# New order tables for a one-core hash-bucket attention and gated feed-forward kernel, and a mask kept in SBUF

## The chip, the cores and the metric

The kernel runs on one core of a Trainium2 chip. The time is that of one launch on the device, in microseconds (us): 607.29 us for the kernel before, the median of three runs (607.15 to 607.84). One more run was taken with the profiler on, and every duration below comes from that run.

## The reference

Four batches of eight attention heads, 768 positions, 64 numbers a head. Each query and key gets a 6-bit bucket from the signs of a projection; a query sees only keys of its own bucket. The heads' outputs are laid side by side (512 wide) and go through a gated feed-forward layer.

```
q_bits = (einsum('bhsd,dk->bhsk', q, proj) > 0)       # k likewise; 6 bits make a bucket
mask   = q_bucket[:, :, :, None] == k_bucket[:, :, None, :]
scores = where(mask, q @ k.T / sqrt(D), -1e9)
attn   = exp(scores - max); attn = attn / (sum + 1e-9)
x      = attn @ v, heads side by side                  # (4, 768, 512)
gate   = sigmoid(causal convolution of x over 5 positions, one filter per column)
out    = (gate * (x @ w_val)) @ w_out
```

## The kernel before

**Tiles.** A unit is one head of one batch (32 of them); a unit has six tiles of 128 queries, so there are 192 tiles, and 48 of them make a batch. One main loop (L521 to L560) runs over the tiles k = 0 to 195; it is called the step of tile k below. A step carries the tile through a chain that is spread over several steps.

**The chain of a tile.** TensorE (PE) makes the scores `s` in two pairs of matmuls (L295) into one of two PSUM buffers. VectorE (DVE) takes the negated row maximum `nm` (L301) and from it the factor `gs` (L307) and the shift `nb` (L311). ScalarE (ACT) makes `p` = exp (L317), with the row sum beside it; that frees the buffer of `s`. For two tiles at a time DVE adds the sums (L323) and takes the reciprocal `ri` (L327). GpSimd (POOL) scales `p` (L332). PE transposes `p` in six pieces into two PSUM buffers `tp` (L341), and ACT copies them to SBUF as `pt` (L350). With three tiles' `pt` a half of a head is complete; PE multiplies with the values (`av`, L364, one step of the generator is two matmuls), and ACT copies `av` into `x` (L372).

**What hangs on it.** For two heads together DVE rounds `x` to `xh` (L384), POOL takes the rest `xl` (L385), and the convolution runs as one POOL and four DVE instructions (L393, L395). After four pairs ACT makes the gates (L399) and the batch's feed-forward products can start: `val` (L426, 12 matmuls into `m`, in pieces of four) and `outp` (L451, also in pieces of four). They are held before a batch's last two output blocks until the next batch's gates are there (`hold`, L475). For a coming unit POOL rounds queries and keys (`aq` L207, `bq` L210), and once in four units PE makes the sign bits (L242, into a `tp` buffer, read by DVE at L245).

**The weights.** They come as 64-bit floats and are taken apart on DVE by five instructions of 128x512 for each of eight parts (L113, L114, L117, L120, L121), between L106 and L129 on ACT and L132 and L134 on POOL. `m` in these lines is one PSUM tile; ACT's output of L106 lies in the SBUF tile `o`.

**What sets the order.** Every engine executes its own instructions in the order in which the program issues them. That order is written by hand: each step has a string of letters, and each letter issues one piece. S scores of the next tile, M maximum, F factor, H shift, E exp, R and I sums and reciprocal, Z scaling, T transposes, K copy of the transposes of the step before, A one step of `av`, C one of the convolution, G one of the feed-forward products, P one of the preparation of a coming unit, W one of the weights. Tables before: FIRST for steps 0 to 5, EARLY (12 strings, step k takes number k mod 12) up to step 59, LATE (12 strings) from step 60 on. A letter whose generator has nothing left issues nothing. In steps up to 63 no G finds anything: the first batch's gates are not there.

```
 30 START = 60
522 o = FIRST[k] if k < 6 else EARLY[k % 12] if k < START else LATE[k % 12]
561 accs[:] = [(ps_m, "m"), (ps_t, "tp"), (ps_s, "s"), (ps_t, "tp"), (ps_s, "s")]
```

After the last step the products of the last batch run alone (L561 to L568), with more PSUM buffers.

Of the kernel before, what the change touches and what calls it, by code (L numbers as in the profile page):

```python
# [11 lines left out]
ALU = mybir.AluOpType  # L12
# [3 lines left out]
I32 = mybir.dt.int32  # L16
U32 = mybir.dt.uint32
# [9 lines left out]

START = 60  # L30
FIRST = ["SGKMRIWFWGTHWWEZ", "GMFRGHSICKWCEGZT", "MSRFIKHETZP",
         "RMSGCKIFCPHTEPGWPCZCPC", "MRFPSCKHEPGIPZCATGPAP", "ASAARAPMWPCFGIHCPKETZ"]
EARLY = ["MRFHCIKSETZ", "MRWIFKHEWGASGCGZT", "MRFKPSHPIPEPATZ",
         "RMKCIFHSAEZT", "MKFPHRIPPEPSCWWZWPTA", "MRFAKHSIWCPETZ",
         "MKRFISPPHEZWT", "MRFHSKAIZWACET", "MSGKCRFIHGWEATZG",
         "MRKIZFSAGCHACTEG", "MAFRIKHGSCWEPPPWPTZ", "MKRFSHPEIAZTW"]
LATE = ["MRKCAAFHISZECGT", "PMSRFPKHGIEATZW", "MFRWHISZCKEGGWWWT",
         "MWSWRICFKHEPPGAAZAPT", "MKFRSIZHCEPCPPGT", "SMFHKRIWWWZCCPGWWECT",
         "MWRPWFAHKIAEASTZ", "MSFWWKRHGEITWZ", "MFRKIHSPCEGWZWGTW",
         "MSRKAAPFIAHGZET", "MFKRSIHGZET", "PSMFKHRIEWCTPZ"]  # L40


@with_exitstack
def kernel(
# [10 lines left out]
    nc = tc.nc  # L55
# [53 lines left out]
    def from_float64(w, m, t):  # L109

        lo, hi = w[:, :, 0], w[:, :, 1]
        a, d, ti = hi.bitcast(FP32), lo.bitcast(FP32), t.bitcast(I32)
        nc.vector.tensor_scalar(out=t, in0=m, scalar1=LEAST, scalar2=None, op0=ALU.max)  # L113
        nc.vector.tensor_scalar(out=ti, in0=ti, scalar1=3, scalar2=0x3fffffff,  # L114
                                op0=ALU.logical_shift_left, op1=ALU.bitwise_and)
        yield
        nc.vector.scalar_tensor_tensor(out=hi, in0=hi, scalar=-2 ** 30, in1=ti,  # L117
                                       op0=ALU.bitwise_and, op1=ALU.bitwise_or)
        yield
        nc.vector.tensor_scalar(out=ti, in0=hi, scalar1=-2 ** 23, scalar2=None, op0=ALU.bitwise_and)  # L120
        nc.vector.scalar_tensor_tensor(out=d, in0=lo.bitcast(U32), scalar=2.0 ** -52, in1=t,  # L121
                                       op0=ALU.mult, op1=ALU.mult)
        return a, d

# [16 lines left out]
    def load_conv():  # L141
        if conv_w.dtype == mybir.dt.int64:
            w = const.tile([P, NP * KW, 2], I32, name="cw64")
            nc.sync.dma_start(out=w, in_=conv_w.bitcast(I32).rearrange("p (n t) -> p n t", t=2))
            t = const.tile([P, NP * KW], FP32, name="cwt")
            yield
            a, d = yield from from_float64(w, magnitudes(w, const.tile([P, NP * KW], FP32, name="cwm")), t)
            yield
            nc.vector.tensor_tensor(out=cw_sb, in0=d, in1=a, op=ALU.add)
        else:  # L150
            nc.sync.dma_start(out=cw_sb, in_=conv_w)
# [32 lines left out]
    def load_raw(i):  # L184
        if i < len(units):
            b, h = units[i]
            raws[i] = raw.tile([P, S], FP32, name="r")
            nc.sync.dma_start(out=raws[i], in_=qk[b, h])

    def load_values(i):  # L190
        b, h = units[i]
        if h % 2 == 0:
            vts[i] = vp.tile([P, KB, P], FP32, name="vt")
            nc.sync.dma_start(out=vts[i], in_=v[b, h // 2])
        else:
            vts[i] = vts[i - 1]
# [101 lines left out]
    def maxima(k):  # L298
        s = ss[k]
        nm = small.tile([P, 1], FP32, name="nm")  # L300
        nc.vector.tensor_reduce(out=nm, in_=s[:, :, 0:HS], axis=AX.XY, op=ALU.max, negate=True)  # L301
        nms[k] = nm
# [18 lines left out]
    def row_sums(k):  # L321
        sums[k] = small.tile([P, 2], FP32, name="s1")
        nc.vector.tensor_reduce(out=sums[k], in_=ps[k][1], axis=AX.X, op=ALU.add)  # L323
# [185 lines left out]
    with tc.manual_schedule(engines=ENGINES):  # L509
        for i in range(5):  # L510
            load_raw(i)
        load_values(0)
        first_prep()
        weights = [load_conv(), load_weights()]
        preps = [prep(1)]
        step(preps)
        scores(0)
        load_raw(5)
        next(weights[0])
        next(weights[1])  # L520
        for k in range(N + LAG + 1):  # L521
            o = FIRST[k] if k < 6 else EARLY[k % 12] if k < START else LATE[k % 12]
            for act in o:
                if act == "K" and 0 <= k - LAG - 1:
                    keep_transposed(k - LAG - 1)
                elif act == "M" and k < N:
                    maxima(k)
                elif act == "R" and k % 2 == 0 and 0 <= k - 2 < N:
                    row_sums(k - 2)
                elif act == "F" and k < N:  # L530
                    factors(k)
                elif act == "I" and k % 2 == 0 and 0 <= k - 2 < N:
# [95 lines left out]
```

## Time and profile before

| what | value |
|---|---|
| median of three runs | 607.29 us (607.15 to 607.84) |
| the profiled execution's own time | 606.39 us |
| its span, first to last instruction | 604.6 us |
| mean granted TensorE clock | 0.997 |
| instructions | 10636 |
| VectorE, busy share of the span | 68% |
| ScalarE, busy share | 70% |
| GpSimd, busy share | 64% |
| read from HBM, written | 23.12 MB, 6.29 MB |

The page gives the busy time of each engine and the waits between them; further views cut the span into stretches, list one engine's instructions in order of time with the idle time ahead of each, and list the instructions of one source line. In such a list a row is: start in us, duration in us, engine, line, operation, output<-inputs, shape, type, count; in square brackets stands idle time of that engine and what ended it. PE's ends are modelled, and a row's matmuls overlap the next row's, so PE's time is read from one row's start to the next row's start.

### The profile page before, as it was taken

How to read it: one execution, taken by the hardware profiler on the slowest of the kernel's cores; microseconds unless marked ns; L12 is line 12 of the kernel's file. 1: busy time of each engine (PE TensorE's matmuls, PEld its weight loads, DVE VectorE, ACT ScalarE, POOL GpSimd, SP SyncE). 2: the span in 40 equal slices, each digit the busy share in tenths (PEclk: the TensorE clock that was granted, in tenths of full speed). 3: DMA queues.
4: the chain of work that ended last, by engine and by line, in shares of the span. 5: the costliest groups of instructions: out<-in, count | busy, mean ns of one | idle time of the engine just before them, and what ended most of it. 6: DMA issues, size and time to landing. Idle time of an engine off the chain costs nothing.

```text
span 604.6 us, 10636 instructions
## 1 busy us (share of the span) xinstructions
PE 586.0 (97%) x3516; PEld 430.6 (71%) x3516; DVE 411.8 (68%) x1007; ACT 425.4 (70%) x891; POOL 386.1 (64%) x380
## 2 busy tenths in 40 slices
PE   6999999999999999999999999999999999999997
PEld 4766656565677777766667777677758777776886
DVE  5778898989855846776756876468575776654532
ACT  4888988798886677768877676676879676674300
POOL 5558887888947755685846677467764768454322
PEclk9899999999999999999999999999999999999999
DMA  8535454535322253424233333332524222200111
GB/s 288 160 85 140 109 156 118 146 91 142 83 62 77 58 142 101 111 50 139 67 104 85 80 111 89 96 90 58 143 44 115 46 63 65 63 19 1 53 52 52
DMA packets 23413, 56.76 MB, mean 94 GB/s; under 512 B 4312, under 2 KB 4568, under 8 KB 23360
## 3 DMA queue, kind: packets, MB, share of 16 engines
q1 hardware_dynamic: 23072, 55.93, 34.2%
q8 instruction: 28, 0.46, 0.3%
q14 instruction: 25, 0.20, 0.1%
q10 hardware_dynamic: 288, 0.17, 0.1%
HBM read 23.12 MB, written 6.29 MB: 49 GB/s over the span
## 4 chain that ended last, share of the span: by engine, by line
PE 76%; ACT 9%; DVE 5%; issue 4%; POOL 4%; DMA 2%; SPq 0%; POOLq 0%; ACTq 0%; DVEq 0%
PE av L364 19%; PE s L295 18%; PE tp L341 15%; PE m L451 8%; PE m L426 8%; ACT p L317 5%; ACT pt L350 2%; DVE nm L301 2%; PE tp L242 2%; DMA r<-in_qk_dram 2%; PE tp L426 1%; PE tp L451 1%; PE s L451 1%; POOL p L332 1%; PE s L426 1%
## 5 line engine op out<-in xcount | busy, mean ns | idle before, releaser
L332 POOL TENSOR_SCALAR p<-p,ri 128x768 f32<-128x768 f32 x192 | 199.8, 1049 | 94.7 <-ACT pt L350 39.4
L301 DVE TENSOR_REDUCE nm<-s 128x1 f32<-128x768 f32 x192 | 183.1, 953 | 81.2 <-PE s L295 80.8
L317 ACT ACTIVATE p<-s,nb,gs 128x768 f32<-128x768 f32 x192 | 192.5, 1003 | 39.0 <-DVE nb L311 32.4
L350 ACT COPY pt<-tp 128x384 f32<-128x384 f32 x384 | 165.4, 485 | 75.9 <-PE tp L341 74.4
L341 PEld LDWEIGHTS tp<-ident,p 128*128 128x128 f32 x1152 | 133.3, 141 | 43.1 <-issue 19.0
L341 PE MATMUL tp<-ident,p 128*128 128x128 f32 x1152 | 160.9, 276 | 2.3 <-ACT pt L350 1.2
L364 PE MATMUL av<-pt,vt 128*64 128x384 f32 x768 | 147.9, 499 | 0.0
L295 PE MATMUL s<-ak,aq 76*128 76x384 f32 x384 | 117.0, 385 | 10.8 <-ACT p L317 9.1
L295 PE MATMUL s<-bk,bq 128*128 128x384 f32 x384 | 99.7, 341 | 0.0
L364 PEld LDWEIGHTS av<-pt,vt 128*64 128x64 f32 x768 | 48.6, 136 | 58.9 <-issue 55.8
L295 PEld LDWEIGHTS s<-ak,aq 76*128 76x128 f32 x384 | 58.0, 190 | 42.2 <-ACT p L317 20.8
L437 POOL TENSOR_TENSOR hl<-ht,hh 128x384 fp32r<-128x384 f32 x32 | 33.6, 1050 | 67.0 <-DVE hh L435 67.0
L395 DVE SCALAR_TENSOR_TENSOR g<-x,cw_sb,g 128x768 f32<-128x768 f32 x64 | 71.9, 1123 | 2.6 <-POOL g L393 2.1
L295 PEld LDWEIGHTS s<-bk,bq 128*128 128x128 f32 x384 | 70.6, 191 | 0.0
L210 POOL TENSOR_TENSOR bq<-r,aq 128x768 fp32r<-128x768 f32 x31 | 57.4, 1852 | 0.9
L385 POOL TENSOR_TENSOR xl<-x,xh 128x384 fp32r<-128x384 f32 x32 | 31.8, 1012 | 30.6 <-DVE xh L384 24.5
L451 PE MATMUL m<-wo,hh 128*128 128x512 f32 x144 | 47.5, 399 | 0.0
L426 PE MATMUL m<-xh,wv 128*128 128x384 f32 x200 | 43.8, 343 | 0.2 <-DVE ht L431 0.2
L311 DVE TENSOR_SCALAR nb<-nm,gs 128x1 f32<-128x1 f32 x192 | 40.3, 210 | 4.5
L317 ACT ACTIVATION_READ_ACCUMULATOR p<-s,nb,gs 128x1 f32 x192 | 38.9, 202 | 0.0
L372 ACT COPY x<-av 64x384 f32<-64x384 f32 x64 | 30.3, 473 | 12.1 <-PE av L364 11.2
L426 PEld LDWEIGHTS m<-xh,wv 128*128 128x128 f32 x200 | 35.2, 188 | 4.3 <-DVE s L323 3.0
(92 smaller groups left out, 468.0 us busy)
## 6 DMA issues: line engine op xcount, KB each, us to landing
r<-in_qk_dram SPq DMA_DIRECT2D x32, 384.0 KB
vt<-in_v_dram SPq DMA_DIRECT2D x16, 384.0 KB
ak<-aq SPq DMA_DIRECT2D x31, 192.0 KB
bk<-aq SPq DMA_DIRECT2D x31, 192.0 KB
bk<-bq SPq DMA_DIRECT2D x31, 192.0 KB
bq<-aq SPq DMA_DIRECT2D x31, 192.0 KB
out_dram<-o SPq DMA_DIRECT2D x23, 256.0 KB
w<-in_w_val_dram SPq DMA_DIRECT2D x4, 512.0 KB
```

The costliest lines, as they stand in the source:

```text
L210: nc.gpsimd.tensor_tensor(out=bq, in0=r, in1=aq.bitcast(FP32), op=ALU.subtract)
L295: nc.tensor.matmul(out=s[:, hf, 0:HS], lhsT=lq[0:n, qs], rhs=rk[0:n, hf * HS:(hf + 1) * HS], start=n == M, stop=n == P)
L301: nc.vector.tensor_reduce(out=nm, in_=s[:, :, 0:HS], axis=AX.XY, op=ALU.max, negate=True)
L311: nc.vector.tensor_scalar(out=nbs[k], in0=nms.pop(k), scalar1=gs[k], scalar2=None, op0=ALU.mult)
L317: nc.scalar.activation(out=p, in_=s[:, :, 0:HS], func=AF.Exp, bias=nb, scale=gs.pop(k), accum_out=sm[:, k % 2, 0:1])
L332: nc.gpsimd.tensor_scalar(out=p, in0=p, scalar1=rcs.pop(k), scalar2=1.0, op0=ALU.mult, op1=ALU.mult)
L341: nc.tensor.transpose(out=tp[:, n * P:(n + 1) * P], in_=p[:, kb * P:(kb + 1) * P], identity=ident)
L350: nc.scalar.copy(out=pt[:, :, qo:qo + P], in_=tp[:, 0:HS].rearrange("p (a b) -> p a b", b=P))
L364: nc.tensor.matmul(out=av[s * D:(s + 1) * D, 0:HS], lhsT=vt[:, kb, hh * D:(hh + 1) * D], rhs=pt[kb // 3][:, kb % 3, :], start=(kb == 0), s ...
L395: nc.vector.scalar_tensor_tensor(out=g, in0=x[:, k:k + S], scalar=w, in1=g, op0=ALU.mult, op1=ALU.add)
L426: nc.tensor.matmul(out=acc[:, 0:HS], lhsT=wv[wi][:, c, j * P:(j + 1) * P], rhs=xs_[(c, o)][xi], start=(m == 0), stop=(m == 11))
L451: nc.tensor.matmul(out=acc, lhsT=hs[(o, j)][hi][:, tb * P:(tb + 1) * P], rhs=wo[wi][:, j, :], start=(m == 0), stop=(m == 11))
```

## The change

All four tables' strings are new. A fourth table, TURN, is taken from step 60 on in the steps with 6 <= k mod 48 < 18, that is steps 60 to 65, 102 to 113 and 150 to 161; LATE holds for the other steps from 60 on. Apart from that, the mask of the weights' exponents (written by L120 and read by L121) goes into the SBUF tile that L106 wrote, no longer into the PSUM tile. The lines of the changed kernel are 5 higher from L120 on (8 higher behind the loop's head).

```diff
-LATE = ["MRKCAAFHISZECGT", "PMSRFPKHGIEATZW", "MFRWHISZCKEGGWWWT",
...
+LATE = ["MAKRFHAPISCEGTZ", "SKWWMRPPFHIGAZEAWWT", "MFSRKHICEGWGWWZT",
...
+TURN = ["MRKWFAHIEPCSZT", "WKSMGRPFHIAPWEZAWWT", "MFRWHCICPKEWPSWWWTZ",
...
-        nc.vector.tensor_scalar(out=ti, in0=hi, scalar1=-2 ** 23, scalar2=None, op0=ALU.bitwise_and)
-        nc.vector.scalar_tensor_tensor(out=d, in0=lo.bitcast(U32), scalar=2.0 ** -52, in1=t,
+        nc.vector.tensor_scalar(out=m.bitcast(I32), in0=hi, scalar1=-2 ** 23, scalar2=None, op0=ALU.bitwise_and)
+        nc.vector.scalar_tensor_tensor(out=d, in0=lo.bitcast(U32), scalar=2.0 ** -52, in1=m,
                                        op0=ALU.mult, op1=ALU.mult)
...
-            o = FIRST[k] if k < 6 else EARLY[k % 12] if k < START else LATE[k % 12]
+            if k < START:
+                o = FIRST[k] if k < 6 else EARLY[k % 12]
+            else:
+                o = TURN[k % 12] if 6 <= k % 48 < 18 else LATE[k % 12]
```

The work is the same on every engine: no instruction is added or taken away. What moves is shown at three places. On PE the rows of step k are here those from its scores (of tile k + 1) up to the next scores.

**Place one, PE, steps 114 to 116** (steps 6, 7 and 8 of LATE's twelve; `s` are scores, `tp` transposes, `m<-xh,wv` and `m<-xl,wv` pieces of `val`). Before:

```order
L295 MATMUL s<-ak,aq 128x384 x2
L295 MATMUL s<-bk,bq 128x384 x2
L341 MATMUL tp<-ident,p 128x128 x6
L295 MATMUL s<-ak,aq 128x384 x2
L295 MATMUL s<-bk,bq 128x384 x2
L426 MATMUL m<-xh,wv_126 128x384 x4
L341 MATMUL tp<-ident,p 128x128 x6
L295 MATMUL s<-ak,aq 128x384 x2
L295 MATMUL s<-bk,bq 128x384 x2
L426 MATMUL m<-xh,wv_127 128x384 x4
L426 MATMUL m<-xl,wv_126 128x384 x4
L341 MATMUL tp<-ident,p 128x128 x6
```

Now:

```order
L300 MATMUL s<-ak,aq 128x384 x2
L300 MATMUL s<-bk,bq 128x384 x2
L431 MATMUL m<-xh,wv_126 128x384 x4
L346 MATMUL tp<-ident,p 128x128 x6
L300 MATMUL s<-ak,aq 128x384 x2
L300 MATMUL s<-bk,bq 128x384 x2
L431 MATMUL m<-xh,wv_127 128x384 x4
L346 MATMUL tp<-ident,p 128x128 x6
L300 MATMUL s<-ak,aq 128x384 x2
L300 MATMUL s<-bk,bq 128x384 x2
L431 MATMUL m<-xl,wv_126 128x384 x4
L346 MATMUL tp<-ident,p 128x128 x6
```

The three pieces of `val` stood as none, one and two between the scores and the transposes of the three steps, and stand as one, one and one. The same happens at steps 66, 78, 90, 126, 138, 162, 174 and 186 with pieces of `val` or `outp`. A step that holds scores and transposes alone on PE is called bare below. From step 60 on there were 25 bare steps and are 16: the nine named here and step 61 are gone, and step 152, whose piece of `outp` moved, is new.

**Place two, DVE and POOL, steps 33 to 37** (EARLY; `g<-x` is the convolution, `xh` the rounding of `x`, `w` a part of the weights). DVE, from the maximum of tile 33 on. Before:

```order
L301 TENSOR_REDUCE nm<-s 128x1
L307 TENSOR_SCALAR gs<-nm 128x1
L395 SCALAR_TENSOR_TENSOR g<-x,cw_sb,g 128x768
L384 CAST xh<-x 128x384 x2
L311 TENSOR_SCALAR nb<-nm,gs 128x1
L301 TENSOR_REDUCE nm<-s 128x1
L307 TENSOR_SCALAR gs<-nm 128x1
L323 TENSOR_REDUCE s_1334<-sm_118 128x2
L327 RECIPROCAL ri<-s_1334 128x2
L311 TENSOR_SCALAR nb<-nm,gs 128x1
L120 TENSOR_SCALAR m<-w_1129 128x512
L121 SCALAR_TENSOR_TENSOR w_1129<-w_1129,m 128x512
```

Now:

```order
L306 TENSOR_REDUCE nm<-s 128x1
L312 TENSOR_SCALAR gs<-nm 128x1
L316 TENSOR_SCALAR nb<-nm,gs 128x1
L400 SCALAR_TENSOR_TENSOR g<-x,cw_sb,g 128x768
L389 CAST xh<-x 128x384 x2
L306 TENSOR_REDUCE nm<-s 128x1
L312 TENSOR_SCALAR gs<-nm 128x1
L328 TENSOR_REDUCE s_1338<-sm_118 128x2
L316 TENSOR_SCALAR nb<-nm,gs 128x1
L332 RECIPROCAL ri<-s_1338 128x2
L125 TENSOR_SCALAR o<-w_1121 128x512
L126 SCALAR_TENSOR_TENSOR w_1121<-w_1121,o 128x512
```

The shift `nb` of tile 33 stood behind a convolution instruction and two roundings, and stands in front of them; so it does in every step 9 of twelve in EARLY, and in step 3 of twelve it now stands in front of one convolution instruction. L120 now writes `o` and L121 reads it (L125 and L126 now). POOL at the same place, from the scaling of tile 32 (before) and of tile 32 (now) on; each `p<-p,ri` is the scaling of one tile. Before:

```order
L332 TENSOR_SCALAR p<-p,ri 128x768
L207 CAST aq<-r 128x768
L332 TENSOR_SCALAR p<-p,ri 128x768
L132 TENSOR_TENSOR w_1129<-w_1129,wv_126 128x512
L332 TENSOR_SCALAR p<-p,ri 128x768
L134 TENSOR_TENSOR wv_127<-w_1129 128x512
L393 TENSOR_SCALAR g<-x,cw_sb 128x768
L332 TENSOR_SCALAR p<-p,ri 128x768
L210 TENSOR_TENSOR bq<-r,aq 128x768
L368 MEMSET x 128x4
```

Now:

```order
L337 TENSOR_SCALAR p<-p,ri 128x768
L137 TENSOR_TENSOR w_1121<-w_1121,wv_126 128x512
L212 CAST aq<-r 128x768
L337 TENSOR_SCALAR p<-p,ri 128x768 x2
L139 TENSOR_TENSOR wv_127<-w_1121 128x512
L215 TENSOR_TENSOR bq<-r,aq 128x768
L398 TENSOR_SCALAR g<-x,cw_sb 128x768
L337 TENSOR_SCALAR p<-p,ri 128x768
L373 MEMSET x 128x4
```

The subtraction `bq` of 128x768 moved one scaling ahead: between two scalings there now stand the weights' L134 (L139), `bq` and the convolution's first product, where L134 and the product stood alone.

**Place three, PE, steps 109 to 111** (TURN; `tp<-r,proj_sb` are the sign bits, `av` attention times values). Before:

```order
L295 MATMUL s<-ak,aq 128x384 x2
L295 MATMUL s<-bk,bq 128x384 x2
L364 MATMUL av<-pt,vt 64x384 x2
L341 MATMUL tp<-ident,p 128x128 x6
L295 MATMUL s<-ak,aq 128x384 x2
L295 MATMUL s<-bk,bq 128x384 x2
L341 MATMUL tp<-ident,p 128x128 x6
L295 MATMUL s<-ak,aq 128x384 x2
L295 MATMUL s<-bk,bq 128x384 x2
L242 MATMUL tp<-r,proj_sb 32x384 x8
```

Now:

```order
L300 MATMUL s<-ak,aq 128x384 x2
L300 MATMUL s<-bk,bq 128x384 x2
L369 MATMUL av<-pt,vt 64x384 x4
L346 MATMUL tp<-ident,p 128x128 x6
L247 MATMUL tp<-r,proj_sb 32x384 x8
L300 MATMUL s<-ak,aq 128x384 x2
L300 MATMUL s<-bk,bq 128x384 x2
L346 MATMUL tp<-ident,p 128x128 x6
L300 MATMUL s<-ak,aq 128x384 x2
L300 MATMUL s<-bk,bq 128x384 x2
L369 MATMUL av<-pt,vt 64x384 x6
```

One step of `av` moved from step 107 to step 109, and the eight sign-bit matmuls from step 111 to the end of step 109, ahead of step 110's scores. At steps 157 to 159 the same rows stand. At steps 59 to 63 one step of `av` moved from 59 to 61, and the sign bits from 63 to either side of step 61's transposes.

More of the change, by code (lines that the diff above doesn't have):

```diff
@@ L30 @@
 START = 60
[L31 to L36, printed above, removed]
-LATE = ["MRKCAAFHISZECGT", "PMSRFPKHGIEATZW", "MFRWHISZCKEGGWWWT",
-         "MWSWRICFKHEPPGAAZAPT", "MKFRSIZHCEPCPPGT", "SMFHKRIWWWZCCPGWWECT",
-         "MWRPWFAHKIAEASTZ", "MSFWWKRHGEITWZ", "MFRKIHSPCEGWZWGTW",
-         "MSRKAAPFIAHGZET", "MFKRSIHGZET", "PSMFKHRIEWCTPZ"]
+FIRST = ["KRGGAGMCTIFHESZGG", "CMWRICKFHWETSWZG", "RCTMIWKFCWCSPCWPHZCWWEW",
+            "TMRFKIHESPPPZ", "RPMFTIAKAPASAAZGPHEPPPCPCPP", "MSRTIFWHCCKEZ"]
+EARLY = ["MFRHSKECGTIZG", "RWMAFIHKESPTCWZ", "MRFKHPISPEPPAPTZ",
+            "KMRFIHSTECZ", "KMFRHIEWPGAPZWWSPWPTPW", "MGRSGFGGGHIKACETZ",
+            "MGPRSFKGIHGZTE", "MRFHSGAIAKAWECZT", "MRKSFIHEPATGCZW",
+            "KMRIFSHAZAETACCP", "MFKRHIGWSEPZWGTPP", "MRKFHWIPGSPAETZ"]
+LATE = ["MAKRFHAPISCEGTZ", "SKWWMRPPFHIGAZEAWWT", "MFSRKHICEGWGWWZT",
+            "SWMKRIFHPWWEPAAPAPCGPWZT", "MKFRPSGHIPECTZ", "SRMKWFHWWIWPPWGPZWECWWT",
+            "MRKAFWPAHEIASGZTW", "SPWKMFRPPHIGETZ", "MRFKHPSIEWCGZT",
+            "SRKMFAACIPHZPGET", "MSKRFHIGETZ", "SKRIMFHECWTZ"]
+TURN = ["MRKWFAHIEPCSZT", "WKSMGRPFHIAPWEZAWT", "MFRWHCICPKEWPSWWWTZ",
+            "MSRFKIHCEPPPAAWAPPTZ", "MSRKFHICECGCTZ", "MRFSHWWKCWPWIWCWGCWPEWZCWT",
+            "MFRKAHIAEAGSTZ", "MKFSPPWRHIPEWTZ", "MFRHKGCEISZGWT",
+            "MKRSAAPFIAWPCHGEZT", "SMFGWRHIKWETZ", "MRPKGSFHIETZ"]
 @with_exitstack
```

## Prediction, made blind

> **What bounds the kernel now.** I read the page's first part, then the busy time by stretches, then the list of PE in order of time.
>
> ```profile
> PE 586.0 (97%) x3516; PEld 430.6 (71%) x3516; DVE 411.8 (68%) x1007; ACT 425.4 (70%) x891; POOL 386.1 (64%) x380
> ...
> 33.00:152.50 119.50, 116.04 (x697) 74.57 (x695) 108.42 (x258) 103.36 (x222) 94.72 (x93) 1.00 0.47 125
> ...
> 305.00:416.00 111.00, 111.00 (x690) 84.96 (x683) 71.51 (x180) 78.42 (x165) 68.67 (x66) 1.00 0.35 91
> ```
>
> A row of stretches has its length, then busy time of PE, PE's weight loads, DVE, ACT and POOL. Two different kernels lie in one span. From 305 to 416 us PE is busy all the 111.00 us and DVE 71.51: PE is the bound, and only time that PE loses there can be won. From 33 to 152.5 us (steps 12 to 58, EARLY) no feed-forward products exist yet; DVE has 108.42 of 119.50 us, PE's busy time is stretched by waits, and DVE is the bound.
>
> DVE's own waits in the early stretch, from the view of waits cut to it:
>
> ```profile
> DVE nm L301 <- PE s L295: 4.2, 10, 0.5
> DVE s L323 <- ACT p L317: 2.4, 9, 0.4
> ```
>
> So 6.6 us is what reordering alone could win there. Since PE hardly stands idle by its own busy time, its losses are read from start to start.
>
> **Part one: bare steps (place one).**
>
> ```profile
> 181.37 0.85 PE L341 MATMUL tp<-ident,p 128*128 128x128 f32 x6
> 182.64 0.62 PE L295 MATMUL s<-ak,aq 76*128 76x384 f32 x2 [0.42 <-ACT p L317]
> ...
> 318.97 0.62 PE L295 MATMUL s<-ak,aq 76*128 76x384 f32 x2
> 319.43 0.52 PE L295 MATMUL s<-bk,bq 128*128 128x384 f32 x2
> 319.79 0.81 PE L341 MATMUL tp<-ident,p 128*128 128x128 f32 x6
> 320.36 0.59 PE L295 MATMUL s<-ak,aq 76*128 76x384 f32 x2
> ...
> 321.85 0.82 PE L341 MATMUL tp<-ident,p 128*128 128x128 f32 x6
> 322.61 0.62 PE L295 MATMUL s<-ak,aq 76*128 76x384 f32 x2
> ...
> 535.13 0.82 PE L341 MATMUL tp<-ident,p 128*128 128x128 f32 x6
> 535.88 0.62 PE L295 MATMUL s<-ak,aq 76*128 76x384 f32 x2
> ```
>
> From the start of six transposes to the start of the next scores PE needs 320.36 - 319.79 = 0.57 us when nothing is late. The bare step 114 takes 320.36 - 318.97 = 1.39 us of PE, and in the step behind it the same stretch is 322.61 - 321.85 = 0.76: PE waits 0.19 for a score buffer. The reason is ACT's pace:
>
> ```profile
> 321.48 0.99 ACT L317 ACTIVATE p<-s,nb,gs 128x768 f32<-128x768 f32 x1
> 323.19 1.01 ACT L317 ACTIVATE p<-s,nb,gs 128x768 f32<-128x768 f32 x1
> ```
>
> From exp to exp ACT takes 323.19 - 321.48 = 1.71 us with no wait between, more than the 1.39 of a bare step. Step 115, with one piece of `val`, takes 322.61 - 320.36 - 0.19 = 2.06 us; with one piece in each of the three steps none is shorter, and ACT keeps up. Of the nine bare steps that vanish I count eight with a wait: 182.64 - 181.37 - 0.57 = 0.70 at the first (step 67's transposes) and about 0.19 at seven others, the last at 535.88 - 535.13 = 0.75. Together 0.70 + 7 x 0.19 = 2.0 us, won in stretches where PE is the bound, so nothing is late next but PE itself. The new bare step 152 gives some back: from nothing to the 0.70 of the first; I take 0.3.
>
> **Part two: the turns (place three).**
>
> ```profile
> 158.56 0.81 PE L341 MATMUL tp<-ident,p 128*128 128x128 f32 x6
> 159.99 0.61 PE L295 MATMUL s<-ak,aq 76*128 76x384 f32 x2 [0.62 <-ACT p L317]
> ...
> 301.10 0.52 PE L295 MATMUL s<-bk,bq 128*128 128x384 f32 x2
> 302.07 0.84 PE L341 MATMUL tp<-ident,p 128*128 128x128 f32 x6 [0.45 <-ACT pt L350]
> 303.34 0.61 PE L295 MATMUL s<-ak,aq 76*128 76x384 f32 x2 [0.43 <-ACT p L317]
> 304.24 1.50 PE L242 MATMUL tp<-r,proj_sb 128*32 128x384 f32 x16
> ...
> 300.46 0.96 ACT L372 COPY x<-av 64x384 f32<-64x384 f32 x2
> 301.44 0.86 ACT L350 COPY pt<-tp 128x384 f32<-128x384 f32 x2
> ```
>
> At step 60 PE loses 159.99 - 158.56 - 0.57 = 0.86 us in a run of three bare steps; now a step of `av` and the sign bits stand in step 61 and the run is broken. I take 0.9 us, of 0 to the 1.5 of the bits. At step 110 the scores' end waits for the transposes 302.07 - 301.10 = 0.97 where 319.79 - 319.43 takes 0.36, and then the scores 1.27 instead of 0.57: 0.61 + 0.70 = 1.3 us, behind which the sign bits still had to come. Putting them into that hole would win 1.3, but they need the two `tp` buffers. ACT frees these with the copies that start at 301.44 and take 0.86, behind the two copies into `x` at 300.46. So the second half of the bits can start at about 302.3, less the 0.64 by which the moved `av` step (the 1.51 of eight rows less the 0.87 of four, below) lets ACT begin earlier, and the transposes behind them wait for DVE to read the bits, behind two convolution instructions. I work that out as step 111's scores starting 0.6 to 1.0 us later than now, with 1.5 us of bits (the row of L242) no longer behind them, and take 0.4 us won at each of the two turns (0 to 1.3). Part two: 0.9 + 0.8 = 1.7 us.
>
> **Part three: the early order (place two).**
>
> ```profile
> 66.99 0.87 PE L364 MATMUL av<-pt,vt 128*64 128x384 f32 x4
> 72.62 1.31 PE L364 MATMUL av<-pt,vt 128*64 128x384 f32 x4
> 76.04 1.51 PE L364 MATMUL av<-pt,vt 128*64 128x384 f32 x8
> 87.77 1.93 PE L364 MATMUL av<-pt,vt 128*64 128x384 f32 x8
> ...
> 87.01 1.50 DVE L395 SCALAR_TENSOR_TENSOR g<-x,cw_sb,g 128x768 f32<-128x768 f32 x1
> ...
> 89.26 0.99 ACT L317 ACTIVATE p<-s,nb,gs 128x768 f32<-128x768 f32 x1 [0.73 <-DVE nb L311]
> ```
>
> The shift of tile 33 waits behind 1.50 us of convolution and two roundings, and ACT stood 0.73 us for it. ACT's copies come late, and with them PE's next transposes: the row of eight `av` ahead of them stretches to 1.93 from 1.51 (76.04), 0.42 us. In step 27 it is 1.31 for 0.87, 0.44 us. With the shift ahead both should go: 0.42 in three rounds and 0.44 in two (the others are small) are 2.2 us, from nothing, if DVE's own work still sets the pace, to the 6.6 us of DVE's waits. What DVE moved behind the shift is late next: `xh` feeds POOL, which waits for it now.
>
> POOL pays:
>
> ```profile
> 68.89 0.91 POOL L332 TENSOR_SCALAR p<-p,ri 128x768 f32<-128x768 f32 x1
> 69.76 1.82 POOL L210 TENSOR_TENSOR bq<-r,aq 128x768 fp32r<-128x768 f32 x1
> ...
> 70.85 0.87 PE L341 MATMUL tp<-ident,p 128*128 128x128 f32 x6
> ```
>
> At step 26 the scaling of a tile ends at 69.80 and its transposes start at 70.85. With `bq` (1.82 us) ahead of it the scaling ends at 71.6, 0.75 us late; the weights' instruction, `bq` and the convolution's product then stand in one row. In rounds with sign bits PE comes 1.5 us later to that place and nothing is lost. Two rounds at half of it: I take 0.75 us lost, of 0 to 4 x 1.82 = 7.3.
>
> **Part four: the mask.**
>
> ```profile
> L120 DVE TENSOR_SCALAR m<-w x8: 683/698/711, 46.6 to 152.0; 128x512 int32<-128x512 int32 x8
> L121 DVE SCALAR_TENSOR_TENSOR w<-w,m x7: 687/690/690, 47.3 to 137.4; 128x512 f32<-128x512 uint32 x7
> L384 DVE CAST xh<-x x8: 347/348/1167, 57.6 to 149.9; 128x384 fp32r<-128x384 f32 x8
> L395 DVE SCALAR_TENSOR_TENSOR g<-x,cw_sb,g x12: 1018/1115/1621, 71.3 to 148.2; 128x768 f32<-128x768 f32 x12
> ...
> 33.00:152.50 119.50, 3.38 (x8) 1.00 0.47 125
> 33.00:152.50 119.50, 14.66 (x12) 1.00 0.47 125
> ```
>
> No row shows the new forms. The nearest to L120 with SBUF on both sides is L384: 3.38 / 8 = 0.42 us a piece in this stretch for 384 columns, 0.56 by length for 512, a little less if part of it is fixed: I take 0.52, of 0.35 (its shortest) to the 0.70 of now. The nearest to L121 is L395, which also reads two SBUF tensors: 14.66 / 12 = 1.22 us for 768 columns, by length 0.81 for 512, against 0.69 now. So 0.18 won and 0.12 lost, 0.06 a weight, 0.4 us for seven weights. The best is 0.35 x 7 = 2.4 us, with L121 as now; the worst is a rival below. The PSUM tile comes free earlier, but no row shows anyone waiting for it: nothing.
>
> The Trainium skill, "SBUF — State Buffer", section "Who interferes with whom", speaks against this edit: a DVE instruction with two SBUF inputs, or in a mode that takes both ports, contends with GpSimd for the shared ports, and the loser blocks. The trace agrees in kind (1621 and 1167 ns at most, against 1018 and 347 at least), but the means above, 1.22 and 0.42 us, show a long wait to be rare; the fifth rival is that rule at its full price. Its "VectorE: DVE Perf Modes", section on the perf-mode tier table, gives one-source fp32 work in SBUF two elements a cycle; by its cycle counts L120 would take an estimated 0.42 us and the sum be 0.7 us lower. The trace leans that way, with 0.9 ns a column in L384's median and 1.36 in L120's.
>
> **Part five: small ones.** PE's order has 97 groups of `av` for 96. By the rows of part three two groups of four take 2 x 0.87 and one of eight 1.51: 0.2 us lost. The first 33 us are reordered as well; I found no row there that decides, give them nothing and leave them to the range.
>
> **The sum**, against the profiled execution's own time of 606.39 us (span 604.6): -2.0 + 0.3 - 1.7 - 2.2 + 0.75 - 0.4 + 0.2 = -5.05, so 601.3. The median stands 0.9 above that execution (607.29), which gives 602.2 us.
>
> **The rivals.**
> First, the early gains come to nothing, since DVE's 108.42 us set that stretch's pace whatever the order: then -2.0 + 0.3 - 1.7 + 0.2 = -3.2, 604.1 us. For it: DVE's busy share there. Against: 6.6 us of waits exist. Chance 0.20.
> Second, the early order closes all of DVE's 6.6 us of waits: -9.8, 597.5 us. Against: waits at other steps of twelve keep their order. 0.10.
> Third, the change does not do what it says: the waits move. A bare step that is filled empties ACT's lead elsewhere, as with the new step 152, and what the turns win is lost behind the sign bits, whose buffers are late: 607.0 us. For it: PE has the same work and the waits are the ring's, not a letter's. 0.12.
> Fourth, slower: POOL's row of three in EARLY. If every round is late by the whole `bq`, 7.3 us go and the early gain with it: -3.2 + 7.3 = +4.1, 611.4 us. It decides the sign from 1.1 us a round on ((3.2 + 1.2) / 4). For it: 0.75 us is worked out for one round already. 0.07.
> Fifth, slower: the port. If L120 and L121 wait as the longest rows of L384 and L395 did (0.82 and 0.60 us over the shortest), 7 x 1.4 = 10.0 us go on the engine that is the bound: 614.1 us; from 0.63 us a weight on it is slower. 0.04.
>
> **How the numbers follow.** The forecast, all four gains at their size, has the rest, 0.47; it is 602.2 us, itself between 600 and 604. A measurement of this kernel tells about 0.2%, 1.2 us, from no change. Forecast and the first two rivals are faster by more: 0.77. The third is within: 0.12. The last two are slower: 0.11. The range leaves out the slower rivals and half of the second: 597.5 to 607.5.
>
> **What would show it.** In the changed kernel's PE list, the stretch from transposes to scores at the steps 7 of twelve behind 180 us should be 0.57 throughout (part one). At steps 109 to 111 the bits should stand where the 1.3 us of waits stood, and the next scores follow at 0.57 or little more (two). In the early stretch ACT's waits for `nb` at step 9 of twelve should be gone, PE's rows of eight `av` matmuls be 1.5 us, and POOL should not end the waits of the transposes (three). L125 should take about 0.5 us and L126 about 0.8, and the early stretch be shorter by some 2 us (three and four). It is wrong if the early stretch is as long as before, if POOL's scaling releases the transposes at step 2 of twelve, or if new waits of 0.5 us stand behind the steps 150 to 153.

## The result and the profile after

The changed kernel takes 611.62 us (median of five executions, 610.30 to 614.17), where five of the kernel before gave 607.29 (606.95 to 607.84): a ratio of 1.0083, 95% interval 1.0066 to 1.0101. It is slower by 4.3 us by the medians and 5.0 by the ratio, where 5 less were forecast. Its profiled execution took 613.11 us, with a span of 611.3.

From the page of the changed kernel, the busy time of the engines and the granted clock in 40 slices; then the row of the early stretch and of a feed-forward stretch from the view of stretches (columns as before, the granted clock behind POOL):

```profile
PE 587.3 (96%) x3516; PEld 431.4 (71%) x3516; DVE 415.1 (68%) x1007; ACT 425.7 (70%) x891; POOL 380.5 (62%) x380
...
PEclk9899999798999999999999999999999999999999
...
33.00:152.50 119.50, 111.68 (x655) 71.78 (x654) 106.57 (x241) 95.76 (x209) 90.76 (x88) 0.96 0.44 114
305.00:416.00 111.00, 110.24 (x690) 84.28 (x689) 72.89 (x183) 80.67 (x169) 70.07 (x68) 1.00 0.35 91
```

The work is the same, and from 305 to 416 us PE is nearly as busy as before (110.24 us for 111.00). In the early stretch PE has done less in the same 119.5 us (111.68 for 116.04), and so has every other engine: the stretch has become longer. Its clock is 0.96 for 1.00, since from 114.9 to 121.8 and from 149.1 to 152.5 us PE was granted half speed, in pieces of 3.41 us. I compare the start of each tile's row maximum on VectorE in the two traces: tile 12 is 0.7 us late, tile 42 2.0, tile 45 5.2, tile 57 8.0, tile 60 8.1; from there to the end 1.4 us are won back. **The loss lies wholly ahead of tile 60, in FIRST and EARLY.** The half clock explains a part of this profiled execution only: another execution of the changed kernel, with a mean clock of 0.997, still took 611.62.

The largest loss lies between tiles 42 and 45, 3.2 us, and the next, 1.8 us, between tiles 54 and 57. These are the convolutions just ahead of the first of them, first VectorE, then GpSimd, at steps 41 and 43; steps 53 and 55 show the same (convolutions of 1.87 and 2.05 us):

```profile
110.68 1.87 DVE L400 SCALAR_TENSOR_TENSOR g<-x,cw_sb,g 128x768 f32<-128x768 f32 x1
116.40 2.06 DVE L400 SCALAR_TENSOR_TENSOR g<-x,cw_sb,g 128x768 f32<-128x768 f32 x1
...
110.69 1.04 POOL L139 TENSOR_TENSOR wo<-w 128x512 fp32r<-128x512 f32 x1
115.83 1.81 POOL L215 TENSOR_TENSOR bq<-r,aq 128x768 fp32r<-128x768 f32 x1
```

L400, the convolution, takes 1.01 us at step 39, where nothing of GpSimd's runs beside it. Here it takes 1.87 beside the weights' addition L139 and 2.06 beside the subtraction L215 (`bq`), both of which read two SBUF tensors as it does: 0.86 and 1.05 us more.

### The profile page after: what moved, and what is told of

The parts are those of the page before. It is cut to its first block, busy times and chain, and to the rows that moved or that the text cites. A ratio compares the mean times of both kernels' runs of the same rounds, so it can differ in the third digit from the quotient of the medians.

```text
span 611.3 us, 10645 instructions
## 1 busy us (share of the span) xinstructions
PE 587.3 (96%) x3516; PEld 431.4 (71%) x3516; DVE 415.1 (68%) x1007; ACT 425.7 (70%) x891; POOL 380.5 (62%) x380
## 4 chain that ended last, share of the span: by engine, by line
PE 77%; DVE 8%; ACT 7%; issue 3%; POOL 3%; POOLq 0%; ACTq 0%; DVEq 0%
PE av L369 20%; PE s L300 18%; PE tp L346 16%; PE m L456 8%; PE m L431 8%; ACT p L322 4%; DVE nm L306 3%; ACT pt L355 2%; PE tp L247 1%; PE tp L431 1%; PE tp L456 1%; PE s L456 1%; DVE g L400 1%; POOL p L337 1%; PE s L431 1%
## 5 line engine op out<-in xcount | busy, mean ns | idle before, releaser
L337 POOL TENSOR_SCALAR p<-p,ri 128x768 f32<-128x768 f32 x192 | 196.9, 1033 | 103.6 <-DVE ri L332 47.0
L400 DVE SCALAR_TENSOR_TENSOR g<-x,cw_sb,g 128x768 f32<-128x768 f32 x64 | 73.9, 1155 | 2.2 <-POOL g L398 2.1
L215 POOL TENSOR_TENSOR bq<-r,aq 128x768 fp32r<-128x768 f32 x31 | 57.5, 1856 | 0.8
```

The source lines that it names most:

```text
L215: nc.gpsimd.tensor_tensor(out=bq, in0=r, in1=aq.bitcast(FP32), op=ALU.subtract)
L337: nc.gpsimd.tensor_scalar(out=p, in0=p, scalar1=rcs.pop(k), scalar2=1.0, op0=ALU.mult, op1=ALU.mult)
L400: nc.vector.scalar_tensor_tensor(out=g, in0=x[:, k:k + S], scalar=w, in1=g, op0=ALU.mult, op1=ALU.add)
```

## The experiments

Every kernel ran beside the kernel before on the same chip; its median there was 606.4 to 606.9 us, so the ratio is what to compare. The intervals in brackets are of 95%. "Before + X" is the kernel before with X alone.

### Which part costs: four kernels

r1, mask alone (before +):

```diff
-        nc.vector.tensor_scalar(out=ti, in0=hi, ...
+        nc.vector.tensor_scalar(out=m.bitcast(I32), in0=hi, ...
```

> The kernel before, with the mask edit alone. Theory A (the new EARLY order costs the time: the weights' two POOL instructions in a row, the late scaling and what follows, with slow-clock stretches behind it): 607.0 to 608.5 us, L126 slower but hidden. Rival B (the mask costs it: two SBUF inputs on VectorE collide with GpSimd): 609.5 to 611.5 us, with L126 near 1.3 us in most of its eight rows.

606.98 us, ratio 0.9995 (0.9978 to 1.0011): nothing that this run can tell from zero.

r2, all tables and the old mask: the changed kernel with the two lines of r1 turned back.

> The changed kernel with the mask back in PSUM: the new tables alone. Theory A: 609.5 to 612 us, as slow as the changed kernel or nearly so. Rival B: 603 to 605.5 us, the gain of the later tables without the mask's cost.

608.63 us, 1.0033 (1.0017 to 1.0049).

r3, before + the new LATE and TURN (the second string of TURN ends in AWT, not in AWWT as the change was printed above); r4, before + the new EARLY:

```diff
-LATE = ["MRKCAAFHISZECGT", "PMSRFPKHGIEATZW", "MFRWHISZCKEGGWWWT",
+LATE = ["MAKRFHAPISCEGTZ", "SKWWMRPPFHIGAZEAWWT", "MFSRKHICEGWGWWZT",
...
+TURN = ["MRKWFAHIEPCSZT", "WKSMGRPFHIAPWEZAWT", "MFRWHCICPKEWPSWWWTZ",
...
```

> The kernel before with the new LATE and TURN alone (old FIRST and EARLY, mask in PSUM). Both theories: faster, 604 to 606 us (the trace of the changed kernel wins 1.4 us from tile 60 to the last, of 3.2 forecast). If the later tables lose as well: 607 us or more.

605.55 us, 0.9971 (0.9953 to 0.9989).

```diff
-EARLY = ["MRFHCIKSETZ", "MRWIFKHEWGASGCGZT", "MRFKPSHPIPEPATZ",
+EARLY = ["MFRHSKECGTIZG", "RWMAFIHKESPTCWZ", "MRFKHPISPEPPAPTZ",
...
```

> The kernel before with the new EARLY alone (old FIRST, old LATE, mask in PSUM). Theory A: 610 to 613 us, all of the loss and none of the later gain. Rival B: 605.5 to 607.5 us. A third theory, that FIRST is to blame: 607 us here.

608.94 us, 1.0034 (1.0020 to 1.0049). So LATE and TURN win 1.3 to 1.8 us, EARLY loses 2, the mask by itself nothing; but with the tables it costs 3 us (611.62 against 608.63). The parts don't add.

### Does the mask cost beside the new early order, and is it GpSimd's order?

r5 is r4 and r1 together; r6 is before + the new FIRST; r8 is the changed kernel with the old FIRST and EARLY. r7 is the changed kernel with two letters moved, which leaves the order of PE, VectorE and ScalarE as it is and moves `bq` and L139 behind the next scaling on GpSimd:

```diff
-"RWMAFIHKESPTCWZ"
+"RWMAFIHKESTCWZP"
...
-"KMFRHIEWPGAPZWWSPWPTPW", "MGRSGFGGGHIKACETZ"
+"KMFRHIEWPGAPZWSPWPTPW", "MGRSGFGGGHIKACETZW"
```

> The kernel before with the new EARLY strings and the mask in SBUF, FIRST, LATE as before, no TURN. Theory A (the mask costs only beside the new early order, some 3 us of it): 611 to 612.5 us, that is 4 to 5.5 above the kernel before, and half-clock pieces between 100 and 152 us. Rival B (the parts simply add; the mask costs nothing and what is missing lies in the first six steps): 608.9 us, as the early order alone.

612.06 us, 1.0098 (1.0074 to 1.0121): 3.1 us above r4 by the medians, 3.9 by the ratios. The interaction is there without LATE, TURN or FIRST.

> The kernel before with the new FIRST strings alone. Theory A: within 1 us of the kernel before (605.9 to 607.9). Rival B: the first six steps cost what the sum lacks, 609 to 610 us, and the maximum of tile 12 starts 2 us or more late.

607.95 us, 1.0022 (1.0010 to 1.0035): between the two expectations; FIRST costs some 1.3 us. Its profile has half clock from 14.6 to 24.8 us, the kernel before from 15.7 to 19.1.

> The changed kernel with the old FIRST and EARLY: the new LATE and TURN and the mask in SBUF stay. Theory A and rival B both: 605.0 to 606.2 us, as with LATE and TURN alone, since the mask costs nothing in the old early order. If it comes at 607 or more, the mask has a price of its own that its run alone hid.

605.20 us, 0.9980 (0.9972 to 0.9988): as expected, and faster than both kernels of the case.

> The changed kernel with GpSimd's order alone put back at two places of EARLY: the subtraction bq of 128x768 behind the next scaling at step 1 of twelve, and the weights' addition L139 behind the scaling of step 5 of twelve. The order on the other three engines is the changed kernel's. Theory A (GpSimd's instructions in a row are what delays the scaling, and so the transposes): 608 to 609.5 us, 2 to 3.5 below the changed kernel. Rival C (the loss comes from the order of VectorE and ScalarE in EARLY, GpSimd only fills its time): 611 to 612 us, no gain.

611.20 us, 1.0073 (1.0059 to 1.0086): no gain that can be told from the noise, so theory A in this form falls. The number is its rival's, whose reason, the order of VectorE and ScalarE, this run does not test. VectorE and GpSimd in r7, at steps 29 and 31:

```profile
80.43 1.65 DVE L400 SCALAR_TENSOR_TENSOR g<-x,cw_sb,g 128x768 f32<-128x768 f32 x1
85.92 2.19 DVE L400 SCALAR_TENSOR_TENSOR g<-x,cw_sb,g 128x768 f32<-128x768 f32 x1
...
80.36 0.91 POOL L337 TENSOR_SCALAR p<-p,ri 128x768 f32<-128x768 f32 x1
85.48 1.81 POOL L215 TENSOR_TENSOR bq<-r,aq 128x768 fp32r<-128x768 f32 x1
```

L139 is out of the convolution's way, and a scaling has taken its place; `bq` stands as before. So the question was no longer what stands in a row on GpSimd, but what starts beside a convolution. The same place in r4, which is 3 us faster than r5, VectorE and then GpSimd:

```profile
78.57 1.01 DVE L395 SCALAR_TENSOR_TENSOR g<-x,cw_sb,g 128x768 f32<-128x768 f32 x1
83.53 1.17 DVE L395 SCALAR_TENSOR_TENSOR g<-x,cw_sb,g 128x768 f32<-128x768 f32 x1
...
78.66 1.82 POOL L134 TENSOR_TENSOR wv<-w 128x512 fp32r<-128x512 f32 x1
83.86 2.52 POOL L210 TENSOR_TENSOR bq<-r,aq 128x768 fp32r<-128x768 f32 x1
```

In r5 the four are:

```profile
79.92 1.87 DVE L396 SCALAR_TENSOR_TENSOR g<-x,cw_sb,g 128x768 f32<-128x768 f32 x1
85.64 2.06 DVE L396 SCALAR_TENSOR_TENSOR g<-x,cw_sb,g 128x768 f32<-128x768 f32 x1
...
79.93 1.04 POOL L135 TENSOR_TENSOR wv<-w 128x512 fp32r<-128x512 f32 x1
85.07 1.81 POOL L211 TENSOR_TENSOR bq<-r,aq 128x768 fp32r<-128x768 f32 x1
```

**The instructions and their order are the same; VectorE's lead is not.** In r4 VectorE starts 0.08 us ahead (the trace's unrounded starts are used for leads): it takes 1.01, and GpSimd 1.82 for 1.04. In r5 it is ahead by 0.02 and loses all the same: it takes 1.87, and GpSimd its 1.04. The lost 0.06 us fit the new mask, which stands on VectorE a little ahead and takes 0.77 us for 0.70: from its start the convolution follows after 2.72 us where it was 2.64, and the addition after 2.73 in both kernels. The loser ends 0.8 to 0.9 us behind the winner. Then, in r5, `bq` comes early as well, ahead of the next convolution, and that one loses too. GpSimd has time to spare, and VectorE by the busy times has little.

In the early stretch r5 loses this race at steps 29, 41 and 53; the changed kernel's profiled execution won it at 29, by 0.03 us, and lost the other two. The twelve convolutions of steps 27 to 57 add up to 14.66 us in the kernel before, 15.37 in r4, 17.31 in the changed kernel and 19.00 in r5, so r5 has 3.6 us more of VectorE than r4, about what it is slower. In the old order, in the kernel before and in r1, no addition starts nearer than 0.25 us to a convolution.

The new EARLY loses one such race without the mask's help. At step 41 of r4, VectorE and then GpSimd:

```profile
109.64 1.73 DVE L395 SCALAR_TENSOR_TENSOR g<-x,cw_sb,g 128x768 f32<-128x768 f32 x1
...
109.52 1.04 POOL L134 TENSOR_TENSOR wo<-w 128x512 fp32r<-128x512 f32 x1
```

The addition starts 0.13 us ahead, the convolution takes 1.73 us and the next one 2.06. From tile 42 to 45 r4 loses 0.65 us, so a part of EARLY's own cost can come from here; no run took this race alone out of r4.

### Turning the race round

r9 and r10 put a small instruction ahead of one of the two. r9 is the changed kernel with this, where `nudge` is an SBUF tile of its own of 128x4:

```diff
+            nc.gpsimd.memset(nudge, 0.0)
             nc.gpsimd.tensor_tensor(out=lo, in0=a, in1=d, op=ALU.add)
```

> The changed kernel with one instruction more for each part of the weights: GpSimd clears 128x4 numbers of a tile of its own (about 0.10 us, the row of the clearing of x) ahead of the addition L139. The theory by now (who starts first): at steps 5 and 7 of twelve in EARLY VectorE's convolution and a GpSimd instruction with two SBUF inputs start within 0.1 us of each other, and the later of the two is held until the other has ended; with the mask in SBUF VectorE comes some 0.1 us later and loses 0.86 us a time, on the engine that is late. Then 0.1 us more on GpSimd gives VectorE the lead back: convolutions of 1.0 to 1.2 us at steps 29, 31, 41, 43, 53 and 55, additions L139 of 1.8 us, no half clock between 100 and 152 us, and 607.5 to 609.3 us, faster for an instruction more. Rival D (the mask's own 0.1 us a weight is multiplied by the chain in another way, GpSimd has no part in it): 611 to 612.5 us, as the changed kernel.

611.73 us, 1.0094 (1.0062 to 1.0127).

r10 is r4 with this ahead of the convolution, `nudge` being 128x96:

```diff
+                    if 24 <= k < 60 and k % 12 == 5:
+                        nc.vector.memset(nudge, 0.0)
```

> The kernel before with the new EARLY strings alone, the old mask, and one instruction more on VectorE: it clears 128x96 numbers of a tile of its own (some 0.1 us) ahead of the convolution at steps 29, 41 and 53. By who starts first: VectorE loses to L134 and then to bq, convolutions of 1.9 and 2.05 us there, and 611 to 613 us with no change of the mask, where the early order alone took 608.9. Rival D: 609 to 609.4 us, by three times the instruction's own 0.1.

608.54 us, 1.0025 (1.0007 to 1.0044). r9 came out as its rival had it and r10 as if nothing had been added, but neither instruction turned a race round. GpSimd and VectorE in r9:

```profile
80.00 1.31 POOL L138 TENSOR_TENSOR w<-w,wv 128x512 f32<-128x512 f32 x1 [0.86 <-ACT wv L135]
81.25 0.10 POOL L140 MEMSET nudge<- 128x4 f32 x1
81.39 1.04 POOL L141 TENSOR_TENSOR wv<-w 128x512 fp32r<-128x512 f32 x1
...
81.37 1.88 DVE L402 SCALAR_TENSOR_TENSOR g<-x,cw_sb,g 128x768 f32<-128x768 f32 x1
```

The clearing lay in the gap between L138 (which ends at 81.31) and the addition: that starts 0.08 us behind L138's end, as it does without a clearing. VectorE led by 0.02 us and lost. In r10 the convolution's row starts 0.01 us ahead of the addition's at step 29 and 0.02 behind it at step 53, so the lead of 0.08 that the expectation of r14 speaks of is gone by the rows; still VectorE won both times (0.92 us, the addition 1.81), and its row ended as early as in r4, counted from the addition's start. So both were made again with a longer clearing: r13 as r9 with 128x192, r14 as r10 with 128x256.

> The changed kernel; ahead of each addition L139 GpSimd clears 128x192 numbers of a tile of its own. The clearing of 128x4 in the run before lay in the 0.08 us between two GpSimd instructions and moved nothing: L139 still started 24 ns behind the convolution, and the convolution took 1.88 us. By the rows so far VectorE loses with a lead of 27 ns or less and wins with 30 ns or more, so L139 has to come some 0.1 us later, which this clearing does. By who starts first: convolutions of 1.0 us at steps 29, 41 and 53 and of 1.2 at 31, 43 and 55, no half clock between 100 and 152 us, and 607.5 to 609.3 us, against 611.6. Rival D (GpSimd has no part in it): 611 to 613 us, and still slow where convolutions are short.

608.14 us, 1.0014 (0.9993 to 1.0036): 3.5 us faster than the changed kernel by the medians, 4.2 by the ratios, with eight instructions more, and no slower than r2, the tables with the old mask (608.63, 1.0033). VectorE and GpSimd at step 41 of r13:

```profile
113.13 1.01 DVE L402 SCALAR_TENSOR_TENSOR g<-x,cw_sb,g 128x768 f32<-128x768 f32 x1
...
113.00 0.26 POOL L140 MEMSET nudge<- 128x192 f32 x1
113.22 1.82 POOL L141 TENSOR_TENSOR wo<-w 128x512 fp32r<-128x512 f32 x1
```

All six convolutions took 1.01 or 1.18 us, and no half clock was left between 100 and 152 us (r7 had none there either and was slow, so that alone says little). **This is the run that settles the interaction**: r9 and r13 differ in the length of one clearing on GpSimd, an engine that is idle over a third of the time, and by 3.6 us by the medians, 4.9 by the ratios. One thing goes with it that was not intended: the convolutions of steps 27 and 51, beside a scaling, fell from 1.6 us to 1.01 as well, so the gain is not that of the six alone; the twelve add up to 12.62 us.

> The kernel before with the new EARLY strings alone and the old mask; ahead of the convolution at steps 29, 41 and 53 VectorE clears 128x256 numbers of a tile of its own. The clearing of 128x96 in the run before delayed the convolution by 0.01 us only, since it filled the gap behind the row of nb, and VectorE kept its lead of 82 ns. By who starts first, with some 0.2 us more VectorE loses at 29 and 53 as it did at 41 already: convolutions of 1.7 to 1.9 us there and 2.05 us two steps later, and 611 to 613 us without any change of the mask. Rival D: 609.2 to 609.8 us, three times 0.2 above the early order alone (608.9).

609.88 us, 1.0042 (1.0021 to 1.0064): a miss for both. VectorE and GpSimd at step 29:

```profile
79.68 0.27 DVE L550 MEMSET nudge<- 128x256 f32 x1
79.87 0.90 DVE L396 SCALAR_TENSOR_TENSOR g<-x,cw_sb,g 128x768 f32<-128x768 f32 x1
...
79.69 1.97 POOL L135 TENSOR_TENSOR wv<-w 128x512 fp32r<-128x512 f32 x1
```

The clearing itself started ahead of the addition, and GpSimd was held for both instructions of VectorE (1.97 us). VectorE did not lose, so this kernel did not test what it should. That VectorE, delayed, loses without the new mask no experiment showed; step 41 of r4, above, is the nearest row.

### What is left of EARLY, and of the turns

r11 is r4 with one step of `av` back from step 7 of twelve to step 3:

```diff
-"KMRFIHSTECZ"
+"KMRFIHSATECZ"
...
-"MRFHSGAIAKAWECZT"
+"MRFHSGAIKAWECZT"
```

> The kernel before with the new EARLY strings alone, in which one step of av stands again at step 3 of twelve and no longer at step 7, so that step 7 has two as in the old strings. If the row of twelve av matmuls (ScalarE waits 1.8 us behind it for the transposes) is what the new early order costs by itself: 607.0 to 607.9 us, from 608.9, and tile 21 no more than 0.3 us later than in the kernel before. If not: 608.5 to 609.3.

608.32 us, 1.0017 (0.9998 to 1.0037), with executions from 606.17 to 613.82: between the two ranges, and unclear. The reason for it, from r4, ScalarE and PE at step 19:

```profile
53.98 0.86 ACT L350 COPY pt<-tp 128x384 f32<-128x384 f32 x2 [1.84 <-PE av L364]
...
53.08 2.16 PE L364 MATMUL av<-pt,vt 128*64 128x384 f32 x12
```

The new EARLY puts three steps of `av` between the scores and the transposes of step 7 of twelve, where two stood; ScalarE waits 1.84 us behind them for the transposes. In r4 tiles 18 to 21 lose 1.1 us, in r11 0.4. But r11 loses 1.5 us from tile 57 to 60, where r4 loses 0.1, so the two letters take back at one place what they win at the other.

r15 is the changed kernel with the old FIRST, r11's two letters and r13's clearing:

> The changed kernel with the old FIRST, the step of av back from step 7 to step 3 of twelve in EARLY, and the clearing of 128x192 ahead of L139; LATE, TURN and the mask are the changed kernel's. If the loss consists of the three parts (the first six steps 1 to 1.5 us, the row of twelve av 1 to 2, the race for the port 3), what is left is the gain of LATE and TURN: 605 to 606.5 us. If a part is missing: 607.5 us or more.

606.53 us, 0.9981 (0.9958 to 1.0005): 5 us below the changed kernel by the medians, and the gain of LATE and TURN is left by the ratio, though the interval is wide and the median just above the range expected. From tile 18 to 21 it loses 0.4 where r4 lost 1.1, but as in r11 another 1.0 goes at tiles 57 to 60. So the three edits together take back nearly all of the loss; how much of that is the two letters', and whether some of EARLY's stays, is open.

r12 is r8 with the P letters of TURN so placed that the sign bits stand at steps 63, 111 and 159 again:

```diff
-"WKSMGRPFHIAPWEZAWT", "MFRWHCICPKEWPSWWWTZ", "MSRFKIHCEPPPAAWAPPTZ"
+"WKSMGRFHIAWEZAWT", "MFRWHCICKEWSWWWTZ", "MSRFKIHCEPPPPPAAWAPPTZPP"
```

> The changed kernel with the old FIRST and EARLY (605.2 us so far), and with the sign bits of TURN back at steps 63, 111 and 159, behind the scores; the rest of TURN and LATE is new. If bits ahead of the next scores only move the wait (1.3 to 1.6 us from the transposes to the bits where 0.57 is needed): 603.8 to 604.9 us. If the early bits fill a hole as the prediction had it: 605.6 to 607.

605.70 us, 0.9979 (0.9962 to 0.9996), the same as r8: early or late, the bits cost the same. The median lies in the range for bits that fill a hole, by 0.1 us, but r8's ratio of 0.9980 says that nothing was won by them.

## Why the prediction was wrong, by its own steps

**Part four, the mask, is the step that failed most.** Its term was a gain of 0.4 us, with L125 at 0.52 us and L126 at 0.81; in its place the mask cost 3.0 us beside the new tables (changed kernel against r2, by the ratios). Three pairs of the changed kernel, on VectorE:

```profile
62.05 0.41 DVE L125 TENSOR_SCALAR o<-w 128x512 int32<-128x512 int32 x1
62.49 1.28 DVE L126 SCALAR_TENSOR_TENSOR w<-w,o 128x512 f32<-128x512 uint32 x1
...
76.82 0.77 DVE L125 TENSOR_SCALAR o<-w 128x512 int32<-128x512 int32 x1
77.62 0.69 DVE L126 SCALAR_TENSOR_TENSOR w<-w,o 128x512 f32<-128x512 uint32 x1
...
91.93 0.80 DVE L125 TENSOR_SCALAR o<-w 128x512 int32<-128x512 int32 x1
92.77 1.28 DVE L126 SCALAR_TENSOR_TENSOR w<-w,o 128x512 f32<-128x512 uint32 x1
```

A pair takes 1.69, 1.46 or 2.08 us where 1.39 stood: a loss of 0.07 to 0.7 a weight, some 2 us of VectorE in seven. L125 took 0.41 us where it started 0.28 ahead of a scaling on GpSimd, and 0.76 to 0.81 where GpSimd was at work already. That size alone was harmless (r1). What decided was the 0.07 ahead of a convolution. The prediction named the port, weighed it at L125 and L126 only, and took 14.66 us for twelve convolutions as proof that long waits are rare; it did not ask which of the two engines waits, and on what margin. The fifth rival had the right resource at the wrong instructions. The fourth rival's 611.4 us lies next to the measured 611.62, but that is chance: it blamed `bq` in a row on GpSimd and put the mask at a gain, and r7, which breaks the row up, is no faster.

**Part three** forecast 2.2 us won by the shift (its five terms add up to 2.14) and 0.75 lost on GpSimd; EARLY alone lost 2.1 (r4). The mechanism of the gain took place: from the changed kernel, PE's eight `av` at step 33 and ScalarE's exp there:

```profile
89.97 1.64 PE L369 MATMUL av<-pt,vt 128*64 128x384 f32 x8
...
90.32 1.01 ACT L322 ACTIVATE p<-s,nb,gs 128x768 f32<-128x768 f32 x1
```

1.64 us instead of 1.93, and no wait for `nb`. GpSimd's 0.75 came too, as a wait of 0.72 on PE at step 26:

```profile
73.07 0.88 PE L346 MATMUL tp<-ident,p 128*128 128x128 f32 x6 [0.72 <-POOL x L373]
```

Tile 30 is no later against before than tile 24 (1.47 us both), so the two together were worth nothing there. Either VectorE's work sets the pace, as the first rival has it, or gain and loss cancel; no run took them apart. What was not in the sum is the third step of `av` at step 7 of twelve, which the order shows as plainly as the rest, and the race of step 41. How EARLY's 2.1 us divide between these stays open.

**Part five** put the first 33 us at zero for want of a row; FIRST costs about 1.3 (r6). Tile 12 is already 1.6 us late in r6. Ten of its twelve executions have a mean clock of 0.994 or less and took 607.82 us or more, the two at 0.997 and 1.0 took 606.50 and 606.76; 19 of 23 executions of the kernel before on that chip have 0.996 or more. So most of the cost goes with more half clock; what in the new strings brings that is not shown.

**Part one** was right in kind and nearly in size. The transposes and the next scores of steps 115 and 116, PE of the changed kernel:

```profile
327.87 0.82 PE L346 MATMUL tp<-ident,p 128*128 128x128 f32 x6
328.44 0.60 PE L300 MATMUL s<-ak,aq 76*128 76x384 f32 x2
...
329.94 0.82 PE L346 MATMUL tp<-ident,p 128*128 128x128 f32 x6
330.51 0.59 PE L300 MATMUL s<-ak,aq 76*128 76x384 f32 x2
```

0.57 us both times. From one such start to the next, over 0.575 us and summed over all steps outside the turns (72 to 101, 114 to 149, 162 to 191), PE's rows give 3.6 us before and 1.8 now: 1.7 us less, where 2.0 were forecast. The new bare step 152 was put at 0.3 us:

```profile
437.17 0.81 PE L346 MATMUL tp<-ident,p 128*128 128x128 f32 x6
438.55 0.61 PE L300 MATMUL s<-ak,aq 76*128 76x384 f32 x2 [0.57 <-ACT p L322]
```

It costs 438.55 - 437.17 - 0.57 = 0.81 us. A new wait of 0.5 us there was one of the prediction's three signs of being wrong, and the other two came as well: the early stretch is longer, and GpSimd releases the transposes of step 26, above.

**Part two** failed in its second half; the wait of 0.86 us at step 60 is gone (166.63 - 166.06 = 0.57 us from transposes to scores). The turn at step 109, PE of the changed kernel:

```profile
307.71 0.87 PE L346 MATMUL tp<-ident,p 128*128 128x128 f32 x6
309.35 1.50 PE L247 MATMUL tp<-r,proj_sb 128*32 128x384 f32 x16 [0.76 <-ACT pt L355]
310.77 0.62 PE L300 MATMUL s<-ak,aq 76*128 76x384 f32 x2
...
308.82 0.86 ACT L355 COPY pt<-tp 128x384 f32<-128x384 f32 x2
```

The bits start 1.64 us behind the transposes, about 1.0 more than is needed, because ScalarE's two copies out of the `tp` buffers run only from 308.82 to 309.68; at step 157 the stretch is again 1.64 us, and at step 61, where the bits stand on both sides of the transposes, PE waits 0.47 and 0.38. The prediction saw that wait and took it for smaller than the hole it fills; the two are alike (r12). Parts one and two were to bring 3.4 us and brought 1.2 to 1.8 (r8 and r3). With the rows of part one (1.7 won, 0.8 lost at step 152) that leaves 0.3 to 0.9 us for the turns, an estimate, where 1.7 were forecast.

The sum by parts from the ratios: LATE and TURN -1.2, FIRST +1.3, EARLY +2.1, the mask beside EARLY +3.9, together +6.1 us, or +5.5 with r3's -1.8 for LATE and TURN, against 5.0 (4.0 to 6.1) measured.

## What to carry to other kernels

Before an instruction with two SBUF inputs is moved, lengthened or put ahead of another one, list what GpSimd starts within 0.1 us of it, and by how much the critical engine leads: a lead of a tenth of a microsecond can be worth 0.9 us, and an edit of 0.07 us can lose it. Test the edits of a change together as well as alone, and when a race is suspected, lengthen the engine that has slack: that is a cheap test and may be the repair. A filler shorter than the gap between two instructions moves nothing, so look at the row before believing a null result.

## What the runs showed of the hardware

Of a convolution on VectorE and an addition on GpSimd, both with two SBUF inputs, that start together, one runs at full speed and the other is held: 1.01 and 1.82 us in r4, 1.87 and 1.04 in r5. In eight traces they start within 0.15 us of each other, those with a clearing on VectorE just ahead left out. There the convolution won when its row started 0.03 us or more ahead of the addition's, and lost at a lead of 0.017 to 0.027 and where the addition was ahead. Why a small lead is not enough they do not show. With a clearing just ahead (r10, r14) it still won when its row started up to 0.18 us behind the addition's, and lost at 0.26 and 0.42 behind (step 41). The Trainium skill, "SBUF — State Buffer", section "Who interferes with whom", says that issue order, not the shape of the operation, decides who blocks. These rows agree, but for the leads under 0.03 us, where the row that starts first lost. The page was in hand for the prediction, which used the half of the rule on who contends and not the half on who loses.

A GpSimd scaling, with one tensor and a column of scalars, held the convolution too (1.65 us in r7, beside the scaling that had started 0.07 us ahead).

The granted clock fell to a half in the middle of a busy stretch, for one or two pieces of 3.41 us. PE of the changed kernel there:

```profile
113.38 0.88 PE L346 MATMUL tp<-ident,p 128*128 128x128 f32 x6 [0.42 <-POOL p L337]
115.09 1.01 PE L300 MATMUL s<-ak,aq 76*128 76x384 f32 x2 [0.83 <-ACT p L322]
...
116.66 4.11 PE L369 MATMUL av<-pt,vt 128*64 128x384 f32 x12
```

Twelve `av` matmuls took 4.11 us for 2.16, so the stretch behind these waits is paid at half speed. The waits alone do not bring it: r2 has waits of 0.42, 0.26 and 0.83 us at the same place and no half clock there. The Trainium skill, "TensorE: Matmul & The Clock Gate", Part 1, has a free-running window of about 3.4 us and half rate after an idle one. The length agrees, but here PE was never idle for 3.4 us. Which share of a window has to be idle these runs do not show.
